# Polysketch attention and a squared-ReLU layer on one core: another layout for v, the weights loaded as float32 and cast on the chip, the key features on GpSimd

## The chip, the core and the metric

The kernel runs on one core of one Trainium2 chip. Its engines work from queues of their own: TensorE (PE) multiplies matrices into PSUM, VectorE (DVE) and ScalarE (ACT) work element by element and read PSUM, GpSimd (POOL) works element by element on SBUF alone, and SyncE (SP) issues DMAs. An instruction starts when it is first in its engine's queue and what it waits for is done. The metric is the device time of one execution in microseconds (us); lower is better.

## The reference

Four batches with four heads of 1,088 tokens, 32 numbers each; S1 and S2 are 8 x 32.

```python
def phi(x):                                    # 32 numbers -> 64 features
    a = einsum('rd,bhsd->bhsr', S1, x)
    b = einsum('rd,bhsd->bhsr', S2, x)
    return einsum('bhsi,bhsj->bhsij', a, b).reshape(*x.shape[:-1], 64)
q_p, k_p = phi(q), phi(k)
kv  = einsum('bhsf,bhsd->bhfd', k_p, v)        # per batch and head 64 x 32
z   = sum(k_p, axis=2)
num = einsum('bhsf,bhfd->bhsd', q_p, kv)
den = einsum('bhsf,bhf->bhs', q_p, z) + 1e-6
x   = (num / den) as 4352 tokens x 128         # the heads side by side
h   = x @ w_in                                 # 128 x 2048
out = (max(h, 0) ** 2) @ w_out                 # 2048 x 128
```

## The kernel before

**Staging.** The 34 x 32 tokens of a head lie as 32 partitions of 34 tokens, so that a tile of k or q is [128 = 4 heads x 32, 34, 32] and comes with one DMA of 544 KB. v is laid out by tokens instead: four DMAs of 32 partitions bring 8 tokens each per head, and two more the tokens left over. All of these are issued on SP, batch by batch (`load`). The two weights come by DMAs of GpSimd that turn them into bfloat16 on the way (`w_in_sb`, `w_out_sb`); a copy of one element ahead of each makes it wait for the last piece of v of batch 0, and for q of batch 1.

**Keys.** `kT` transposes k in 32 x 32 blocks on DVE, `ka` multiplies by S1 and S2 on PE, `kc` copies the result out of PSUM on ACT, `kp` forms the 64 products of a token on DVE, and `kv` sums products times v over the tokens on PE. `kt` copies the sums to SBUF, `kr` turns them upright with a matmul against the identity, `kx` copies them to `KV`. The tokens of k and of v must be the same in each group of rows: in `kT` row and column follow the layout of v. `kg`, `gs`, `wz` and `wc` give the sums for the denominator.

**Queries.** `qT` transposes q on DVE, `qa` multiplies on PE, `qc` copies; `dt`, `dr`, `da` make the denominator's reciprocal and scale; `qf` forms the products and `qp` transposes them, all on DVE. `nd` multiplies them with `KV` on PE (32 x 32 matmuls, sixteen at a time in the array), and `xe` copies the result as bfloat16, which gives x transposed.

**The layer.** The tokens go in nine chunks, eight of 512 and one of 256 columns. For chunk `ci` and pair `u` of eight, `M` makes two 128 x 512 results of x and w_in in one of two PSUM buffers, `R` takes the ReLU of both (128 x 1024) on ACT or DVE, `S` squares them on DVE or ACT (with `@M` two pairs at once), and `O` adds their products with w_out, eight matmuls of 128 columns, to one PSUM buffer. `E` copies a chunk's result, and four DMAs of SP store it.

**The order.** One text, `ORDER`, lists every operation, as `name.arguments@engine`; `pin` keeps the order of the program, so each engine's queue is the order of its operations in that text. In names here, kp.1.0 is the first half of batch 1, M.0.5 is chunk 0 and pair 5. `W.n` puts n idle matmuls (128 x 128 x 512) into PE's queue; before, the text has none, and eight stand ahead of it in the program.

Of the kernel before, what the change touches and what calls it, by code (L numbers as in the profile page):

```python
# [10 lines left out]
F32 = mybir.dt.float32  # L11
BF16 = mybir.dt.bfloat16
# [58 lines left out]
def kernel(  # L71
# [11 lines left out]
    nc = tc.nc  # L83
# [6 lines left out]
    NLO = 8  # L90
# [49 lines left out]
    for b in range(B):  # L140
        kin_t[b] = kin.tile([128, NJ, D], F32, tag=f"k{b}", name="k_in")
        qin_t[b] = kin.tile([128, NJ, D], F32, tag=f"q{b}", name="q_in")
        vraw[b] = vin.tile([128, H, NLO + 1, D], F32, tag=f"v{b}", name="v_in")


    def load(b):
        for dst, src in ((kin_t, k), (qin_t, q)):
            nc.sync.dma_start(out=dst[b], in_=src[b].rearrange("h (t j) d -> (h t) j d", j=NJ))
        vb = v[b].rearrange("h (t j) d -> t h j d", j=NJ)
        for i in range(4):  # L150
            nc.sync.dma_start(  # L151
                out=vraw[b][32 * i : 32 * (i + 1), :, :NLO, :].rearrange("t h l d -> t h (l d)"),
                in_=vb[:, :, i * NLO : (i + 1) * NLO, :].rearrange("t h l d -> t h (l d)"),
            )
        for j2 in range(2):
            nc.sync.dma_start(
                out=vraw[b][32 * j2 : 32 * (j2 + 1), :, NLO, :], in_=vb[:, :, 4 * NLO + j2, :]
            )


# [4 lines left out]
    w_in_sb = consts.tile([128, d_ff], BF16)  # L165

    pin(nc.gpsimd.tensor_copy(w_in_sb[:1, :1], vraw[0][:1, 0, NLO, :1]))
    nc.gpsimd.dma_start(out=w_in_sb, in_=moe_w_in)

    w_out_sb = consts.tile([128, C_TILES, 128], BF16)  # L170
    pin(nc.gpsimd.tensor_copy(w_out_sb[:1, 0, :1], qin_t[1][:1, 0, :1]))
    nc.gpsimd.dma_start(out=w_out_sb, in_=moe_w_out.rearrange("(c ct) d -> c ct d", ct=C_TILES))
# [91 lines left out]
    def kT(b, i, eng):  # L264
        if i == 0:
            T["kT", b] = kTp.tile([128, S], F32, tag="kT", name="kT")
        kt, src = T["kT", b], kin_t[b]
        l0, l1 = (4 * i, 4 * i + 4) if b == 0 else (0, NLO)
        pin(
            nc.vector.transpose(  # L270
                kt[:, 128 * l0 : 128 * l1].rearrange("p (l h t) -> p l h t", h=4, t=32),
                src[:, : 4 * NLO, :].rearrange("p (h l) d -> p l h d", h=4)[:, l0:l1],
            )
        )
        if b == 0 and i == 0:
            return
        pin(
            nc.vector.transpose(  # L278
                kt[:, 1024:].rearrange("p (j t) -> p j t", j=2), src[:, 4 * NLO :, :]
            )  # L280
        )
# [112 lines left out]
    def kr(b, eng):  # L394
        T["kr", b] = t = ps_m.tile([128, 512], F32, tag="m", name="kr_ps")
        for f in range(2):
            pin(
                nc.tensor.matmul(
                    t[:, 128 * f : 128 * f + 128],
                    T["kvT", b][:, f].rearrange("p c i -> p (c i)"),  # L400
                    ident,
                    start=True,
                    stop=True,
                )
            )
# [207 lines left out]

    def M(ci, u, eng):
        N = columns(ci)
        T["h", ci, u] = t = ps_h.tile([128, 2, 512], F32, tag="h", name="h_ps")
        for i in range(2):
# [3 lines left out]
                    w_in_sb[:, 2 * u + i :: C_TILES],  # L621
# [32 lines left out]
    def O(ci, u, eng):  # L654
# [3 lines left out]
        for i in range(2):  # L658
            ct = 2 * u + i
            for m in range(nt):  # L660
# [4 lines left out]
                        w_out_sb[:, ct, :],  # L665
# [28 lines left out]
    OPS.update(W=W, M=M, R=R, S=SQ, O=O, E=E)  # L694
# [34 lines left out]
```

## Time and profile before

| | us |
|---|---|
| median of the 3 runs (113.83 to 116.07) | 114.15 |
| the profiled execution | 112.86 |
| its span, first to last instruction | 111.1 |
| busy: PE, DVE, ACT, POOL | 98.9, 94.5, 84.3, 2.2 |
| PE from the first M to the last O | 21.1 to 106.8 |
| last O to the end of the span (copy, last DMA) | 4.3 |

A line of a group in the profile reads: line of the kernel, engine, operation, tiles written and read, shapes, count, then the busy time together and the mean of one in ns, then the idle time of the engine ahead of them and what ended it. In a timeline the columns are start, length, engine, line. PE's matmuls are pipelined: what one costs in a row of equals is the distance from start to start and not its length. A line of stages begins with the two ends in us and the length.

### The profile page before, as it was taken

What the parts mean: (1) busy time and instruction counts of PE and PEld (TensorE: products, weight loads), DVE (VectorE), ACT (ScalarE), POOL (GpSimd) and SP (SyncE); (2) the same over time, 40 slices, a digit from 0 to 9 for tenths busy, and PEclk for the clock granted to TensorE, in tenths of its full rate; (3) what the DMA queues carried; (4) which work ended last, traced back from release to release, by engine and by line L of the source; (5) the groups of instructions that cost most, each with busy time, mean ns of one, the idle gap of its engine ahead of it and who ended that gap; (6) DMA issues with size and microseconds to landing.
All of it is one profiled execution on the core that took longest, in us unless ns stands there. A gap on an engine that the chain in (4) does not pass through costs nothing.

```text
span 111.1 us, 4158 instructions
## 1 busy us (share of the span) xinstructions
PE 98.9 (89%) x1817; PEld 77.3 (70%) x1835; DVE 94.5 (85%) x149; ACT 84.3 (76%) x138; POOL 2.2 (2%) x10
## 2 busy tenths in 40 slices
PE   5786788599999999999999999999999999989940
PEld 2165676256868878777788678888767887879830
DVE  5479946975999999999999999999959999988900
ACT  3331023379999999999999997999989779957730
POOL 2000320000000000000000000000000000000000
PEclk9999557959999999999999999999999999999998
DMA  3899999999990000300400003040030021031031
GB/s 96 239 238 213 280 212 304 284 254 210 305 179 3 6 3 6 94 0 6 94 6 0 0 6 94 0 97 3 6 81 13 6 67 27 0 74 32 5 89 53
DMA packets 6691, 10.24 MB, mean 92 GB/s; under 512 B 2193, under 2 KB 4369, under 8 KB 6673
## 3 DMA queue, kind: packets, MB, share of 16 engines
q1 hardware_dynamic: 6224, 8.85, 32.0%
q0 software_dynamic: 288, 1.05, 4.8%
q8 instruction: 14, 0.23, 0.9%
q10 hardware_dynamic: 160, 0.07, 0.2%
q14 instruction: 5, 0.03, 0.1%
HBM read 8.79 MB, written 2.23 MB: 99 GB/s over the span
## 4 chain that ended last, share of the span: by engine, by line
PE 59%; DMA 16%; ACT 14%; issue 3%; SPq 2%; DVE 1%; POOL 0%; ACTq 0%
PE o_ps L662 22%; PE h_ps L619 22%; ACT r_sb L639 10%; DMA w_in_sb<-in_moe_w_in_dram 8%; DMA v_in<-in_v_dram 7%; PE nd_ps L583 3%; PE kab_ps L293 3%; PE qab_ps L447 3%; PE acc_ps L374 3%; ACT g_sb L650 2%; SPq L151 2%; DMA out_dram<-osb 2%; PE h_ps L583 1%; ACT xT L607 1%; ACT osb L674 1%
## 5 line engine op out<-in xcount | busy, mean ns | idle before, releaser
L639 ACT ACTIVATE r_sb<-h_ps 128x1024 bf16<-128x1024 f32 (+1 forms) x67 | 62.8, 1005 | 7.4 <-PE h_ps L619 4.7
L662 PEld LDWEIGHTS <-g_sb 128*128 128x128 bf16 x544 | 34.0, 98 | 8.2 <-issue 0.6
L619 PE MATMUL h_ps<-xT,w_in_sb 128*128 128x512 bf16 (+1 forms) x126 | 37.7, 381 | 2.0 <-DMA w_in_sb<-in_moe_w_in_dram 1.3
L652 DVE TENSOR_TENSOR g_sb<-r_sb 128x1024 bf16<-128x1024 bf16 (+2 forms) x44 | 39.1, 925 | 0.3
L662 PE MATMUL o_ps<-w_out_sb,g_sb 128*128 128x128 bf16 x544 | 38.0, 219 | 0.5
L619 PEld LDWEIGHTS <-w_in_sb 128*128 128x128 bf16 x144 | 16.7, 149 | 5.0 <-issue 2.4
L323 DVE TENSOR_TENSOR kp<-kab 128x1024 f32<-128x1024 f32 (+1 forms) x8 | 10.6, 1336 | 0.0
L551 DVE STREAM_TRANSPOSE qp<-qf 128x1024 f32<-128x1024 f32 (+1 forms) x9 | 10.4, 1175 | 0.2
L538 DVE TENSOR_TENSOR qf<-aq,qab 128x1024 f32<-128x1024 f32 (+1 forms) x9 | 10.4, 1157 | 0.1
L583 PE MATMUL h_ps<-qp,KV 32*32 32x256 f32 (+2 forms) x224 | 8.2, 321 | 0.0
L583 PE MATMUL nd_ps<-qp,KV 32*32 32x256 f32 (+2 forms) x224 | 8.1, 321 | 0.0
L293 PEld LDWEIGHTS kab_ps<-Wk,kT 128*64 128x64 f32 x136 | 5.2, 149 | 2.8 <-issue 1.1
L583 PEld LDWEIGHTS nd_ps<-qp,KV 32*32 32x32 f32 x224 | 5.1, 110 | 2.4 <-DVE g_sb L652 0.8
L293 PE MATMUL kab_ps<-Wk,kT 128*64 128x64 f32 x136 | 6.0, 238 | 0.9 <-DVE kT L278 0.5
L374 PE MATMUL acc_ps<-kp,v_in 128*32 128x64 f32 x288 | 5.8, 244 | 0.9 <-DMA v_in<-in_v_dram 0.9
L374 PEld LDWEIGHTS acc_ps<-kp,v_in 128*32 128x32 f32 x288 | 5.1, 125 | 2.2 <-PE cz_ps L469 1.0
L641 DVE TENSOR_SCALAR r_sb<-h_ps 128x1024 bf16<-128x1024 f32 (+1 forms) x5 | 5.1, 1010 | 0.8 <-PE h_ps L619 0.6
L674 ACT COPY osb<-o_ps 128x512 f32<-128x512 f32 (+1 forms) x9 | 5.2, 581 | 0.6 <-PE o_ps L662 0.5
L417 DVE STREAM_TRANSPOSE qT<-q_in 128x512 f32<-128x512 f32 x8 | 5.2, 682 | 0.3 <-DMA q_in<-in_q_dram 0.3
L270 DVE STREAM_TRANSPOSE kT<-k_in 128x1024 f32<-128x1024 f32 (+1 forms) x5 | 5.0, 1017 | 0.0
L447 PEld LDWEIGHTS qab_ps<-Wq,qT 128*64 128x64 f32 x96 | 4.1, 137 | 1.1 <-issue 0.8
L311 ACT COPY kab<-kab_ps 128x256 f32<-128x256 f32 (+1 forms) x12 | 3.4, 320 | 1.9 <-PE kab_ps L293 1.8
(69 smaller groups left out, 68.8 us busy)
## 6 DMA issues: line engine op xcount, KB each, us to landing
k_in<-in_k_dram SPq DMA_DIRECT2D x4, 544.0 KB, 3.8
q_in<-in_q_dram SPq DMA_DIRECT2D x4, 544.0 KB, 6.8
out_dram<-osb SPq DMA_DIRECT2D x33, 64.0 KB, 1.7
v_in<-in_v_dram SPq DMA_DIRECT2D x16, 128.0 KB, 7.1
w_in_sb<-in_moe_w_in_dram POOLq DMA_DIRECT2D x1, 512.0 KB, 8.7
w_out_sb<-in_moe_w_out_dram POOLq DMA_DIRECT2D x1, 512.0 KB, 9.8
v_in<-in_v_dram SPq DMA_DIRECT2D x8, 16.0 KB, 6.7
out_dram<-osb ACTq DMA_DIRECT2D x1, 64.0 KB
```

Of the source, the lines that this page charges most:

```text
L293: nc.tensor.matmul(kk[64 * c : 64 * c + 64, m * 64 : (m + 1) * 64], kt[:, c0 + 64 * c : c0 + 64 * c + 64], Wk.rearrange("p h x -> p (h x)" ...
L323: tt.tensor_tensor(out=t[:, :n], in0=s[:, 0, :n, :, None].to_broadcast([128, n, r, r]), in1=s[:, 1, :n, None, :].to_broadcast([128, n, r, r]),
L374: nc.tensor.matmul(acc[32 * h : 32 * h + 32, :64], vraw[b][:, h, 4 * gi + m, :], t[:, m * H + h].rearrange("p i j -> p (i j)"), start=(gi ...
L447: nc.tensor.matmul(t[64 * c : 64 * c + 64, m * n : (m + 1) * n], cols, Wk.rearrange("p h x -> p (h x)") if not b else Wq[:, be].rearrange( ...
L538: nc.vector.tensor_tensor(out=t[:, :n], in0=T["aq", b][:, g0 : g0 + n, :, None].to_broadcast([128, n, r, r]), in1=T["qab", b][:, g0 : g0 + ...
L551: nc.vector.transpose(T["qp", b][:, :, 128 * i : 128 * i + 32 * nm].rearrange("p f (m t) -> p m f t", t=32), T["qf", b, i][:, : nm * H].re ...
L583: nc.tensor.matmul(nds[l][32 * h : 32 * h + 32, d0 : d0 + n], KV[rows, be[l // 2], f, 32 * h : 32 * h + 32], src[rows, 2 * h + f, c0 : c0 ...
L619: nc.tensor.matmul(t[:, i, :N], w_in_sb[:, 2 * u + i :: C_TILES], T["x", ci][:, :N], start=True, stop=True,)
L639: pin(nc.scalar.activation(t, h, ACTF.Relu))
L652: pin(nc.vector.tensor_mul(t, s, s))
L662: nc.tensor.matmul(T["o", ci][:, m, :], T["g", ci, u // 2][:, 2 * (u % 2) + i, m * 128 : (m + 1) * 128], w_out_sb[:, ct, :], start=(ct == ...
L674: pin(COPY[eng](osb[:, :nt], T["o", ci][:, :nt]))
```

## The change

- **v.** A head's tokens are taken in 64 runs of 17: two DMAs a batch bring 9 and 8 tokens of each run to partitions 0 to 63 and 64 to 127. `kT` now makes two transposes, each writing every second column, where it made one.
- **Weights.** `w_in` and `w_out` come as float32 on SP, between the loads of batch 1, and are cast in four pieces each by `ci` and `co`: seven on GpSimd, `ci.1` on ACT. GpSimd issues no DMA any more.
- **Key features.** All eight `kp` are on GpSimd.
- **kr.** The two float32 matmuls against the identity are transposes.
- **The order.** `ORDER` is another text: the operations stand elsewhere, seven idle matmuls lie ahead of M.0.0, and some copies, squares and ReLUs change engine: E from nine on ACT to seven and two on DVE, kx from three to one on ACT, S from four to two, R from 67 to 68.

```diff
+wk.0 bp.0 kT.0.0 ka.0.0 kT.0.1 bd.0 kc.0.0 ka.0.1 kc.0.1 W.2 kg.0 qT.0 qa.0.0 gs.0@V wz.0 wc.0
+qc.0.0@V wq.0 W.1 cz.0 dt.0.0 dr.0.0 qa.0.1 qc.0.1@A kT.1.0 da.0.0 cz.1 kp.0.0@G kv.0.0 dt.0.1
+kp.0.1@G W.2 kv.0.1 ci.3@G qf.0.0 qp.0.0 kt.0 ci.0@G ka.1.0 ka.1.1 kc.1.0 kc.1.1 kp.1.0@G kr.0
+kx.0@A kg.1 gs.1@A W.1 nd.0 qT.1 ci.1@A xe.0.0@V xe.0.1@A wz.1 W.1 M.0.0 R.0.0@A M.0.1 dr.0.1
+R.0.1@A wc.1 da.0.1 qf.0.1 qa.1.0 qa.1.1 qc.1.0@A qc.1.1@A kp.1.1@G S.0.0@V ci.2@G M.0.2 R.0.2@A
+M.0.3 R.0.3@A kv.1.0 kv.1.1 kt.1 qp.0.1 nd.1 dt.1.0 xe.1.0@A M.0.4 kT.2.0 ka.2.0 ka.2.1 xe.1.1@A
+co.2@G R.0.4@A co.1@G co.0@G kc.2.0 M.0.5 M.0.6 kc.2.1 dr.1.0 S.0.3@M S.0.1@V O.0.0 R.0.5@A kg.2
...
     def load(b):
         for dst, src in ((kin_t, k), (qin_t, q)):
+            if b == 1 and src is q:
+                nc.sync.dma_start(out=w_in_raw, in_=moe_w_in)
             nc.sync.dma_start(
+                out=dst[b][:, :NJ], in_=src[b].rearrange("h (t j) d -> (h t) j d", j=NJ)
+            )
+        if b == 1:
             nc.sync.dma_start(
+                out=w_out_raw, in_=moe_w_out.rearrange("(c ct) d -> c (ct d)", ct=C_TILES)
+            )
+        vb = v[b].rearrange("h (p l) d -> p h l d", l=17)
+        for c, n in ((0, 9), (1, 8)):
+            nc.sync.dma_start(
+                out=vraw[b][64 * c : 64 * c + 64, :, :n, :].rearrange("p h l d -> p h (l d)"),
+                in_=vb[:, :, 9 * c : 9 * c + n, :].rearrange("p h l d -> p h (l d)"),
+            )
...
-    pin(nc.gpsimd.tensor_copy(w_in_sb[:1, :1], vraw[0][:1, 0, NLO, :1]))
-    nc.gpsimd.dma_start(out=w_in_sb, in_=moe_w_in)
...
+        for j2 in range(2):
+            pin(
+                nc.vector.transpose(
+                    kt[:, 128 * l0 : 128 * l1].rearrange("p (l c t j) -> p j l c t", c=2, j=2, t=32)[:, j2],
+                    src[:, 17 * j2 : 17 * j2 + 18]
+                    .rearrange("p (c l) d -> p l c d", c=2)[:, l0:l1],
+                )
+            )
...
-                nc.tensor.matmul(
+                nc.tensor.transpose(
                     t[:, 128 * f : 128 * f + 128],
                     T["kvT", b][:, f].rearrange("p c i -> p (c i)"),
                     ident,
-                    start=True,
-                    stop=True,
                 )
...
+    def ci(p, eng):
+        src = w_in_raw.rearrange("d (c ct) -> d ct c", ct=C_TILES)
+        pin(COPY[eng](w_in_sb[p], src[:, 4 * p : 4 * p + 4]))
+
+    def co(p, eng):
+        src = w_out_raw.rearrange("c (ct d) -> c ct d", ct=C_TILES)
+        pin(COPY[eng](w_out_sb[p], src[:, 4 * p : 4 * p + 4]))
...
-                    w_in_sb[:, 2 * u + i :: C_TILES],
+                    w_in_sb[u // 2][:, 2 * (u % 2) + i, :],
```

## The prediction

> **What bounds the kernel now.** I read the slices of the span first, then the chain that ended last, then the sums by stage, then the rows of the operations that change place. The slices, forty of 2.78 us each:
>
> ```profile
> PE   5786788599999999999999999999999999989940
> DVE  5479946975999999999999999999959999988900
> ACT  3331023379999999999999997999989779957730
> PEclk9999557959999999999999999999999999999998
> DMA  3899999999990000300400003040030021031031
> GB/s 96 239 238 213 280 212 304 284 254 210 305 179 3 6 3 6 94 0 6 94 6 0 0 6 94 0 97 3 6 81 13 6 67 27 0 74 32 5 89 53
> ```
>
> There are two regimes. Up to about 22 us the DMA engines are full while PE, DVE and ACT wait in turn, with TensorE's clock halved in three slices and at 0.7 in one. From 25 us on the three engines are full together, and the loads end near 33 us. The sums by stage (windows of 5 us) show that ACT is as tight there as PE:
>
> ```profile
> 35.00:40.00 5.00, 4.95 (x62) 4.31 (x62) 4.93 (x9) 5.00 (x9) 0.00 (x0) 1.00 0.02 3
> 60.00:65.00 5.00, 4.85 (x110) 3.60 (x110) 4.96 (x8) 5.00 (x10) 0.00 (x0) 1.00 0.01 3
> ```
>
> The columns after the length are PE, weight load, DVE, ACT, POOL, clock, DMA share and GB/s. A busy PE is not a PE at its peak, so I measure PE by its pitch, read from the chain in order of time where nothing interrupts it:
>
> ```profile
> 73.98 0.44 PE h_ps L619 x2
> 74.42 0.45 PE o_ps L662 x8
> ```
>
> So an M (two matmuls) costs 0.44 and an O (eight) 0.45. In the same way ka costs 0.57 and 0.64 (first and second half of a batch), qa 0.76, kv 1.13 a batch, kr 0.45, kg 0.31, wz 0.2, nd 0.9 (batch 0) to 1.45. In the order written out, what follows M.0.0 is 81.1 us of PE by these prices: M 29.9, O 30.6, ka 3.1, qa 4.8, kv 3.4, kr 1.35, kg 0.9, wz 0.6, nd 6.5. M.0.0 starts at 21.09 and the last O ends at 106.77, so 85.7 were taken and 4.6 lost: about half at the halved clock before M.0.5 (28.59, where 75.7 are left), 2.5 after it. The last copy and its DMA take 4.3.
>
> The start and the queue of loads, from the timeline:
>
> ```profile
> 5.10 0.43 SPq L148 DMA_DIRECT2D k_in<-in_k_dram  x1
> 8.52 0.35 SPq L148 DMA_DIRECT2D q_in<-in_q_dram  x1
> 13.42 0.35 SPq L148 DMA_DIRECT2D k_in<-in_k_dram  x1
> 21.09 1.41 PE L619 MATMUL h_ps<-xT,w_in_sb 128*128 128x512 bf16 x3 [1.30 <-DMA w_in_sb<-in_moe_w_in_dram]
> ```
>
> The loads are issued in order on SP, and an issue waits for the landing of the one eight places earlier: q of batch 1 goes out at 8.52 when q of batch 0 lands, k of batch 2 at 13.42 when k of batch 1 lands. M.0.0 waits 1.30 us for w_in; its x was ready at 19.5.
>
> **What moves off DVE and ACT.** The rows, by shape:
>
> ```profile
> L639 ACT ACTIVATE r_sb<-h_ps 128x1024 bf16<-128x1024 f32 x61 | 59.5, 1045 | 6.2 <-PE h_ps L619 4.2 <-remote 1.6 <-PE acc_ps L374 0.2
> L323 DVE TENSOR_TENSOR kp<-kab 128x1280 f32<-128x1280 f32 x4 | 5.9, 1466 | 0.0
> L323 DVE TENSOR_TENSOR kp<-kab 128x1024 f32<-128x1024 f32 x4 | 4.8, 1206 | 0.0
> L674 ACT COPY osb<-o_ps 128x512 f32<-128x512 f32 x8 | 4.9, 608 | 0.1
> masks.py:199 POOL TENSOR_SCALAR_AFFINE_SELECT ident<-ident 128x128 f32<-128x128 f32 x1 | 0.3, 287 | 0.1
> L167 POOL CAST w_in_sb<-v_in 1x1 bf16<-1x1 f32 x1 | 0.2, 176 | 10.5 <-DMA v_in<-in_v_dram 10.5
> ```
>
> All eight kp leave DVE: 4 x 1.206 + 4 x 1.466 = 10.7 us. DVE takes two E (0.6), two kx, two qc, one xe and two more S, and gives up one R: about +4. ACT loses two E (0.61 each), two kx (0.4), two qc (about 0.45), one xe (0.8), two S (1.09) and gains an R and ci.1. Summed by the new order, ACT's work from M.0.0 to nd.2 (the products of batch 1) falls from 24.0 to 22.5, and from nd.2 to the end from 67.0 to 63.8. These are sums of means; neighbours overlap (61 x 1.045 = 63.7 against 59.5 busy), so I take 0.93 of them. For before this gives 22.3 for M.0.0 to nd.2, and 21.09 to 43.37 were measured: ACT set that stage. After: 20.9.
>
> **On GpSimd.** No row has a product there. From the CAST of one element and the select of 128, one element costs (287 - 176)/127 = 0.87 ns. With that slope once, kp costs 1.07 and 1.29 us; with 287/128 = 2.24 ns an element, 2.30 and 2.87. I take the slope twice, for two inputs: 1.96 and 2.40. A cast of 512 elements is between 0.62 and 1.15 us; I take 0.62, as it is the same operation as the CAST row. The Trainium skill (GPSIMD Engine Reference, Elementwise — side-by-side cycle accounting) gives 4497 ns for a 2048-element product; by it a kp would cost, as an estimate, 2.25 and 2.85, kp.1.1 below would end 0.8 later, still before v1, and the sum would be the same.
>
> **Loads.** All now stand in one SP queue: k0 q0 v0 v0 k1 w_in q1 w_out v1 v1 k2, and so on. With 18 loads on SP instead of 32, the eight-places rule holds w_out only for k0 and k2 only for v0, so nothing is issued late; the bytes decide. Summed over the slices, the kernel before has moved 3.28 MB (k0 to w_in) at 15.4 us, 3.83 (q1) at 17.6, 4.88 (w_out) at 21.2, 5.44 (v1) at 23.2 and 6.0 (k2) at 25.5. Landings come behind their bytes: q0's are reached at 6.1 and it landed at 8.5, v0's at 8.6 and 11.9, k1's at 11.3 and 13.4. With 2.1 to 2.3 us of lag: w_in 17.5, q1 19.7, w_out 23.3, v1 25.5, k2 27.7. Before, q1 landed at 15.6 and k2 at 22.4. The v rows (1,152 and 1,024 bytes against 1,024, the 128-byte pieces gone) I cost at nothing: v0 is needed at 13.7, after kp.
>
> **The new start.** DVE: qT.0 from 8.5 (q0's landing) to 10.1, then gs, wc and qc.0.0 to 11.3, dt.0.0 and dr.0.0 to 12.5. Next stands kT.1.0, waiting for k1 until 13.4; its two 128x512 transposes and the rest (2 x 0.68 + 0.2, against 1.24 + 0.2) end at 15.0. Behind it wait da, dt.0.1, qf.0.0 and qp.0.0 (0.29 + 0.28 + 1.22 + 1.23): 18.0, against 15.1 before. Writes at every second element have no row; a transpose at twice its price would put DVE 1.3 later here, still ahead of q1. PE: kv.0 ends near 16, ka.1 17.2, kr.0 18, nd.0 19.3, where kp on GpSimd (7.0 to 8.9 and to 11.3) is long done. The seven idle matmuls are 0.22 to 0.43 each in gaps and cost nothing. Then qT.1, put ahead of xe.0.0 on DVE, waits for q1: 19.7 + 1.54, xe.0.0 + 0.54, so M.0.0 at 21.9 instead of 21.1. GpSimd, where kp.1.0 and kp.1.1 stand behind ci.3 and so behind w_in too, has cast ci.3 and ci.0 by 18.7 (19.8 at the upper price), so the cast is hidden behind qT.1 and would cost only what it runs past 21.8.
>
> **The next wait.** kv.1 needs v1 (25.5) and kp.1.1 (23.1; 25.0 at the upper price), and PE reaches it at about 25.3, held by ACT's R. O.0.0 needs co.0 (25.6, or 29.6) and comes at about 31. So GpSimd's price doesn't count up to its upper end. ka.2.0 needs kT.2.0: k2 at 27.7 + 1.56 = 29.3, and PE stands idle for about 2 us. After ka.2 (1.2), M.0.5 starts at 30.5. By then the new order has also done qa.1 and kv.1 (1.52 + 1.13), which came after M.0.5, and three kr by transposes save half of 0.45 each (the transpose of L211 has one record where a kr matmul has two): 72.4 us are left. 30.5 + 72.4 = 102.9, against 28.59 + 75.7 = 104.3: 1.4 gained. Of the 2.5 lost after this point in before I take 0.8 away, since ACT has 3 us less to do after nd.2 (bounds 0 and 2.5). **Sum: -2.2 us**, between -1.4 and -3.9. The profiled run took 112.86 (span 111.1 and 1.76 around it), 1.1% below the median 114.15 of the runs shown; I put the difference on the median: **111.9 us**.
>
> **Rivals.** *Loads without the lag.* One queue of few, large pieces may land with its bytes: q1 17.6, k2 25.5. Then M.0.0 comes at 20.2 behind qp.0.0, M.0.5 at 28.3, 3.6 instead of 1.4 gained, and with 0.8 to 2.5 of the later loss 4.4 to 6.1 in all: about 109.2. For it: k0, alone on the engines, landed at 4.5, its bytes being reached at 4.0. Against it: q0, too, was a large piece and lagged 2.4.
>
> *GpSimd and DVE shut each other out* (slower). DVE has only 0.8 us to spare: its sum from M.0.0 to qp.1.1 is 20.0, so 21.8 to 41.8, while PE is ready for nd.2 at 30.5 + 12.1 = 42.6. In that stretch GpSimd has 9.9 us (three kp, five casts) beside S, qf, da and dt, which read two SBUF inputs. If DVE waits for half of it, nd.2 is 4.1 later than forecast: -2.2 + 4.1 = +1.9; if for all, +6.9. It is slower than before once DVE waits for more than 3.0 of the 9.9. No trace of before has both engines at work, so nothing speaks for or against it by a number; it costs 1 to 5% with the middle at +3, 117.2. The Trainium skill (SBUF — State Buffer, Who interferes with whom) has this as a rule: a DVE instruction with two SBUF inputs and a GpSimd instruction that reads SBUF exclude each other for the whole instruction. By that rule the +1.9 to +6.9 would come; no run so far can show it.
>
> *The weights land slowly.* The packets of q1 took 32.0% of the span for 8.85 MB, 4.0 us a MB; the weights' queue q0 4.8% for 2.1 MB read, 2.5. At q1's rate the two weights take 3.1 us more, k2 lands at 30.8, and the sum is +0.9: 115.0.
>
> **How the numbers follow.** Chances: forecast 0.34, loads without lag 0.22, shut-out 0.29, slow weights 0.15. A measurement here tells about 2% (2.3 us). The forecast's own range, 110.3 to 112.8, lies half on each side of that line: faster 0.22 + 0.18 = 0.40; slower 0.19 of the shut-out and 0.05 of slow weights = 0.24; the rest, 0.36, is within 2%. The range runs from 108.0 (loads without lag, all of the loss gone) to 117.2 (the shut-out's middle).
>
> **What would show it.** Right: M.0.0 waits on xT from DVE behind q1, not on w_in; a PE gap of 1 to 2 us before ka.2 that ends with k2; kp on POOL near 2 us; qf and S on DVE at 1.2 as before. Wrong: those two rows longer, or POOL's far above 2.9 (shut-out); q1 before 18 us (no lag); k2 after 30 (slow weights); an ACT still full to 65 us, which would leave the 2.5 us in place.

## The result: 6% slower

| | before | after |
|---|---|---|
| median of the runs, us | 113.99 (4 runs, 113.01 to 116.07) | 121.06 (4 runs, 120.25 to 123.98) |
| the profiled execution; its span | 112.86; 111.1 | 121.58; 119.5 |
| busy: PE, DVE, ACT, POOL | 98.9, 94.5, 84.3, 2.2 | 105.1, 96.1, 82.3, 26.9 |
| M.0.0 starts; M.0.5 | 21.09; 28.6 | 22.17; 38.35 |
| nd.2 starts; nd.4 | 43.37; 62.6 | 50.88; 69.4 |

The kernel after takes 1.0627 times as long as before, with a 95% interval of 1.0495 to 1.0759. (On this core some executions of any kernel take 1.5 to 4% longer than the rest; the ratios here leave them out, and where too few others were left, the range of the runs stands alone.) Of the 8.4 us between the two spans, 7.5 are there when nd.2 starts.

The slices of the kernel after, forty of 2.99 us each, to be laid beside those of before:

```profile
PE   5799997909939999999559999999999999999970
DVE  5362697795992459999999999999997989988740
ACT  4012115623607899989539999999998978997870
POOL 2029444995000980009900000000000000000000
PEclk9999999985595899999999999999999999999997
DMA  3999999999930000030030001301201200303031
```

PE is full sooner than before (from the third digit, the idle matmuls counted), then falls to 0 at the ninth digit, 24 to 27 us, and to 3 at the twelfth; its clock is halved just behind each of these. A second dent, 5 and 5, lies at 57 to 63 us, where ACT falls to 5 and 3 as well, and there the clock is full. These are two different losses.

**The first loss: PE waits, and for nothing that another engine does.** The timeline of PE in the kernel after (start, length, instruction; in brackets the idle time ahead of it and what ended it):

```profile
22.17 1.02 PE L633 MATMUL h_ps<-xT,w_in 128*128 128x512 bf16 x4
23.12 0.88 PE L452 MATMUL qab_ps<-Wq,qT 128*64 128x96 f32 x15
27.06 1.70 PE L452 MATMUL qab_ps<-Wq,qT 128*64 128x96 f32 x17 [3.06 <-issue]
30.52 2.15 PE L381 MATMUL acc_ps<-kp,v_in 128*32 128x64 f32 x72
...
35.26 0.29 PE L588 MATMUL nd_ps<-qp,KV 32*32 32x128 f32 x1 [1.87 <-issue]
```

qa.1 stops after 15 of its matmuls and goes on 3 us later with the same inputs. "issue" says that the profile knows of no semaphore that it waited for. There are three such stops: in ka.1 at 17.54 (1.06 us to the next record), in qa.1 at 23.75 (3.31) and in nd.1 at 33.13 (2.13). In the trace's list of PE's records (weight loads, matmuls and those of its sequencer together) they stand behind records 449, 705 and 961: exactly 256 apart. Queue q8, which the page of the profile calls "instruction", moves its packets of 16,384 bytes just then, and each stop ends 1.4 to 1.5 us after one of them is done. So I read these stops as PE having run out of instructions; the experiments below test it.

From these records, in us. A new block of 256 is entered, and in the same moment the fetch of the next can begin; the fetch's packets start and end; the next block is needed, which is where the last record of the old one starts:

| | entered | fetch | wait to its start | needed | PE stops for |
|---|---|---|---|---|---|
| before | 10.43 | 13.63 to 14.99 | 3.2 | 17.39 | 0 |
| | 17.39 | 20.72 to 21.68 | 3.3 | 25.34 | 0 |
| | 25.34 | 26.77 to 28.05 | 1.4 | 31.75 | 0 |
| after | 12.61 | 16.12 to 17.22 | 3.5 | 17.54 | 1.06 |
| | 18.60 | 24.16 to 25.59 | 5.6 | 23.75 | 3.31 |
| | 27.06 | 32.56 to 33.88 | 5.5 | 33.13 | 2.13 |
| | 35.26 | 36.40 to 37.77 | 1.1 | 43.47 | 0 |

Two things have changed. While the loads run, a block lasts 4.9 to 6.1 us in the kernel after and 6.4 to 8 in before; the new order leaves PE fewer gaps. And the fetch starts later while the loads run: the last load lands at 35.6, and from then on the wait is 1.1 us or less and no stop is left. The Trainium skill (Runtime: NRT & Kernel Launch, Instruction fetch mechanics) has the block of 256 instructions and 16 KiB, which this trace shows, and says that the cost of crossing one is "mostly hidden"; here three crossings cost 6.5 us.

The windows of 5 us behind the stops (PE, weight load, DVE, ACT, POOL, clock, DMA share, GB/s):

```profile
25.00:30.00 5.00, 2.94 (x21) 1.84 (x21) 3.72 (x5) 1.19 (x3) 3.47 (x4) 0.60 1.06 263
30.00:35.00 5.00, 3.39 (x108) 2.36 (x106) 4.93 (x9) 2.08 (x3) 0.00 (x0) 0.72 0.81 152
35.00:40.00 5.00, 4.74 (x73) 3.06 (x74) 1.50 (x4) 3.02 (x9) 0.88 (x1) 0.66 0.02 4
```

The clock is 0.60, 0.72 and 0.66, where before had 0.99, 1.00 and 1.00 in the same three windows. At that clock kv.1 took 2.08 us (1.13 in before) and ka.2 2.12 (1.21), so the stops are followed by a second loss. But the clock was halved for as long in before, 10.2 us in each of the two profiles: at 11.4 to 18.3 and 21.7 to 25.1 there, at 26.0 to 32.8 and 36.3 to 39.7 here. How much of the 8.4 us the clock makes is therefore not shown.

**The second loss: DVE and GpSimd.** Rows by shape (count, busy us, mean ns, idle before), first two of before, then three of the kernel after:

```profile
L652 DVE TENSOR_TENSOR g_sb<-r_sb 128x2048 bf16<-128x2048 bf16 x21 | 24.9, 1205 | 0.0
L525 DVE TENSOR_TENSOR aq<-qab,den 128x256 f32<-128x256 f32 x3 | 1.2, 404 | 0.0
```

```profile
L666 DVE TENSOR_TENSOR g_sb<-r_sb 128x2048 bf16<-128x2048 bf16 x23 | 30.7, 1357 | 4.7 <-ACT r_sb L653 4.6
L530 DVE TENSOR_TENSOR aq<-qab,den 128x256 f32<-128x256 f32 x3 | 2.2, 719 | 0.1
L330 POOL TENSOR_TENSOR kp<-kab 128x1280 f32<-128x1280 f32 x4 | 9.8, 2450 | 20.3 <-issue 20.3
```

A mean hides it; single instructions show it. The timeline of DVE, and that of GpSimd, around the second dent:

```profile
54.31 3.42 DVE L666 TENSOR_TENSOR g_sb<-r_sb 128x2048 bf16<-128x2048 bf16 x1
58.52 1.31 DVE L530 TENSOR_TENSOR aq<-qab,den 128x256 f32<-128x256 f32 x1
```

```profile
8.19 4.32 POOL L330 TENSOR_TENSOR kp<-kab 128x1024 f32<-128x1024 f32 x2 [6.89 <-ACT kab L318]
...
54.05 5.50 POOL L330 TENSOR_TENSOR kp<-kab 128x1280 f32<-128x1280 f32 x2 [9.64 <-issue]
```

The square that begins at 54.31, just behind a kp, takes 3.42 us instead of 1.2. Meanwhile the reduction and the reciprocal on DVE, which have one input, keep their lengths (0.44 and 0.35). GpSimd pays too: the pair of kp takes 4.32 us at the start, where DVE mostly transposes, and 5.50 here. DVE's next ReLU comes late, and PE waits for it, as PE's timeline shows:

```profile
61.02 0.81 PE L633 MATMUL h_ps<-xT,w_in 128*128 128x512 bf16 x3 [2.16 <-DVE r_sb L655]
```

### The profile page after: what moved, and what is told of

It is laid out like the page before. It is cut to its first block, busy times and chain, and to the rows that moved or that the text cites. A ratio compares the mean times of both kernels' runs of the same rounds, so it can differ in the third digit from the quotient of the medians.

```text
span 119.5 us, 4166 instructions
## 1 busy us (share of the span) xinstructions
PE 105.1 (88%) x1834; PEld 74.7 (63%) x1834; DVE 96.1 (80%) x155; ACT 82.3 (69%) x130; POOL 26.9 (23%) x21
## 4 chain that ended last, share of the span: by engine, by line
PE 67%; DVE 20%; issue 6%; DMA 3%; ACTq 0%; ACT 0%
PE h_ps L633 21%; PE o_ps L676 19%; DVE g_sb L666 10%; PE qab_ps L452 5%; PE kab_ps L300 5%; PE acc_ps L381 4%; DVE qp L556 4%; PE nd_ps L588 4%; PE idle_ps L195 3%; DMA S<-in_S_dram 3%; DVE qf L543 2%; PE cz_ps L474 2%; PE h_ps L588 1%; DVE aq L530 1%; PE gg_ps L345 1%
## 5 line engine op out<-in xcount | busy, mean ns | idle before, releaser
L666 DVE TENSOR_TENSOR g_sb<-r_sb 128x2048 bf16<-128x2048 bf16 (+2 forms) x46 | 44.2, 999 | 5.3 <-ACT r_sb L653 5.1
L633 PE MATMUL h_ps<-xT,w_in 128*128 128x512 bf16 (+1 forms) x144 | 40.5, 380 | 2.2 <-DVE r_sb L655 2.2
L676 PE MATMUL o_ps<-w_out,g_sb 128*128 128x128 bf16 x544 | 38.7, 219 | 0.4 <-DVE g_sb L666 0.4
L330 POOL TENSOR_TENSOR kp<-kab 128x1024 f32<-128x1024 f32 (+1 forms) x8 | 19.4, 2448 | 30.4 <-issue 20.3
L633 PEld LDWEIGHTS <-w_in 128*128 128x128 bf16 x144 | 11.9, 100 | 8.8 <-issue 5.7
L452 PE MATMUL qab_ps<-Wq,qT 128*64 128x96 f32 x96 | 5.6, 271 | 3.1 <-issue 3.1
L195 PE MATMUL idle_ps<-idle 128*128 128x512 bf16 x15 | 6.8, 561 | 1.2 <-DVE mask L133 1.2
L300 PE MATMUL kab_ps<-Wk,kT 128*64 128x64 f32 x136 | 7.1, 271 | 0.8 <-issue 0.8
L300 PEld LDWEIGHTS kab_ps<-Wk,kT 128*64 128x64 f32 x136 | 6.3, 181 | 1.7 <-issue 1.0
L276 DVE STREAM_TRANSPOSE kT<-k_in 128x512 f32<-128x512 f32 (+1 forms) x10 | 5.2, 571 | 0.0
```

The source lines that it names most:

```text
L195: pin(nc.tensor.matmul(T["idle"], idle[:, :128], idle, start=True, stop=True))
L300: nc.tensor.matmul(kk[64 * c : 64 * c + 64, m * 64 : (m + 1) * 64], kt[:, c0 + 64 * c : c0 + 64 * c + 64], Wk.rearrange("p h x -> p (h x)" ...
L330: tt.tensor_tensor(out=t[:, :n], in0=s[:, 0, :n, :, None].to_broadcast([128, n, r, r]), in1=s[:, 1, :n, None, :].to_broadcast([128, n, r, r]),
L452: nc.tensor.matmul(t[64 * c : 64 * c + 64, m * n : (m + 1) * n], cols, Wk.rearrange("p h x -> p (h x)") if not b else Wq[:, be].rearrange( ...
L633: nc.tensor.matmul(t[:, i, :N], w_in_sb[u // 2][:, 2 * (u % 2) + i, :], T["x", ci][:, :N], start=True, stop=True,)
L666: pin(nc.vector.tensor_mul(t, s, s))
```

## The experiments

Two theories came out of this: **F**, the fetch of PE's instructions stands late behind the queued loads; and **S**, the shut-out: GpSimd's products and DVE's operations with two inputs exclude each other. The expectations use these letters where they use any. All times are medians in us; the ratio is to the kernel before as it ran beside that kernel, with its 95% interval. Where a range stands in place of a ratio, it is that of the kernel's own four runs, and such a row can't be placed more closely than 2 to 4%. The column of before differs by up to 1.7%, so rows are compared by their ratios.

| kernel | us | before | ratio |
|---|---|---|---|
| after | 121.06 | 113.99 | 1.0627 [1.0495, 1.0759] |
| few_loads_before | 111.66 | 112.41 | 0.9895 [0.9798, 0.9992] |
| few_loads_after | 116.25 | 112.41 | 1.0400 [1.0253, 1.0547] |
| kp_on_dve | 122.96 | 112.41 | runs 119.16 to 124.00 |
| order_alone | 118.09 | 112.41 | 1.0544 [1.0448, 1.0641] |
| kp_gpsimd_before | 125.96 | 113.55 | 1.1042 [1.0862, 1.1221] |
| casting_dma_after | 122.48 | 113.55 | runs 119.26 to 123.54 |
| v17_before | 113.61 | 113.55 | 1.0014 [0.9963, 1.0065] |
| kr_before | 113.36 | 113.55 | runs 110.88 to 114.36 |
| memset_kp_after | 117.38 | 113.76 | 1.0222 [1.0055, 1.0390] |
| small_loads_after | 116.45 | 113.76 | 1.0237 [1.0126, 1.0348] |
| memset_kp_few_loads | 107.97 | 113.76 | 0.9527 [0.9424, 0.9631] |
| small_loads_memset | 111.39 | 114.28 | 0.9831 [0.9740, 0.9921] |
| small_kp23_dve | 116.23 | 114.28 | runs 113.54 to 116.42 |
| small_kp123_dve | 115.62 | 114.28 | 1.0288 [1.0192, 1.0384] |
| before_small | 114.91 | 114.28 | 1.0059 [0.9958, 1.0159] |

### Fewer loads, in both kernels

Both kernels leave out the loads of batches 2 and 3 and compute these from the tiles of batches 0 and 1:

```diff
+        if b >= 2:
+            kin_t[b], qin_t[b], vraw[b] = kin_t[b - 2], qin_t[b - 2], vraw[b - 2]
+            continue
...
-    for b in range(B):
+    for b in range(2):
         load(b)
```

> The changed kernel without the loads of batches 2 and 3 (it computes them from the tiles of batches 0 and 1; 3.3 MB less to load, all else as it was). Theory F: with less queued on the DMA engines the blocks of code come earlier, the pause at 33.1 us goes and that at 23.8 shrinks under 1.5 us, TensorE's clock stays full from 26 us on, the products of batch 2 move from 50.9 to about 45, run 114 to 117. Theory L: nothing of this depends on loads that nobody waits for; run 120 to 122. Theory O (the order itself is at fault): as L.

> The control for the run without the loads of batches 2 and 3: the kernel before, with the same loads left out. Theory F: its blocks of code already arrive in time or behind other waits, so it gains 0 to 1.5 us (112.5 to 114). If it gains as much as the changed kernel does, the loads cost both alike and explain nothing of the difference.

Against before the kernel after falls from 1.063 to 1.040, and before itself to 0.990; the intervals are a point or more wide to each side, so the times alone say little. The profiles say more. PE's stops shrink from 1.06, 3.31 and 2.13 to 0.73, 1.12 and none, and M.0.5 starts at 29.23 instead of 38.35; before has no such stop with its loads or without. F is at work, then, and in the kernel after. But 4.6 us still lie between the two medians. In few_loads_after PE now waits elsewhere; its sum of waits and the timeline of DVE:

```profile
PE o_ps L679 <- DVE g_sb L669: 4.1, 2, 3.8
```

```profile
30.36 2.63 DVE L533 TENSOR_TENSOR aq<-qab,den 128x256 f32<-128x256 f32 x1
33.02 2.87 DVE L546 TENSOR_TENSOR qf<-aq,qab 128x1024 f32<-128x1024 f32 x1
```

Both run beside a pair of kp on GpSimd (30.00 to 34.80), at 6.5 and 2.4 times their lengths in before (0.40 and 1.22), and the squares that O needs stand behind them: S. With the loads gone this pair, the kp of batch 2, ran 9 us earlier than in after, where it had met one square and lengthened it by 0.9.

### The key features back on DVE

```diff
-... kp.0.0@G kv.0.0 dt.0.1 kp.0.1@G ... kp.1.0@G ... kp.1.1@G ... kp.2.1@G ... kp.2.0@G ... kp.3.1@G ... kp.3.0@G
+... kp.0.0 kv.0.0 dt.0.1 kp.0.1 ... kp.1.0 ... kp.1.1 ... kp.2.1 ... kp.2.0 ... kp.3.1 ... kp.3.0
```

> The changed kernel with its eight key products on VectorE again, nothing else moved. Theory L (GpSimd and VectorE shut each other out, and this is what costs): VectorE's long rows go (aq of 128x128 from a mean of 1139 ns back to 290, the squares of 3422 and 2120 ns to 1200), but VectorE takes 10.7 us more; run 118 to 120. Theory F (TensorE waits for its own instructions, because the blocks of code arrive late behind the loads): the pauses of 3.3 us at 23.8 and 2.1 us at 33.1 stay, run 120 to 123.

Its runs (119.16 to 124.00) and those of the kernel after (120.25 to 123.98) overlap: no gain is shown. The order of the kernel after has kp.0.0 behind gs, wc, qc, dt, dr, kT.1.0 and da on DVE's queue, where DVE waits for PE twice (1.50 and 1.37 us); kp.0.0 starts at 15.64, PE stops for 4.31 us ahead of kv.0, and M.0.0 starts at 25.59. This run exchanges one wait for another and can't weigh S by itself. It does show that GpSimd's casts lengthen DVE's operations too: beside those of 13.54 to 16.61 da took 0.82 us and kp.0.0 2.05, where order_alone, which has no casts, had 0.25 and 1.22 in the same place. The stops of F shrink to 1.20 and 1.15, since PE, held up elsewhere, reaches its blocks later.

### One part at a time, in the kernel before

The order alone (kp on DVE, no ci and co, everything else as before):

```diff
-wk.0 wq.0 kT.0.0 ka.0.0 kT.0.1 bp.0 bd.0 kc.0.0 kp.0.0 ka.0.1 kc.0.1 kg.0 gs.0@A qT.0 wz.0 wc.0
+wk.0 bp.0 kT.0.0 ka.0.0 kT.0.1 bd.0 kc.0.0 ka.0.1 kc.0.1 W.2 kg.0 qT.0 qa.0.0 gs.0@V wz.0 wc.0
+qc.0.0@V wq.0 W.1 cz.0 dt.0.0 dr.0.0 qa.0.1 qc.0.1@A kT.1.0 da.0.0 cz.1 kp.0.0 kv.0.0 dt.0.1
...
```

> The kernel before with the new order text alone: its own loads, its weights by casting DMAs, the layout of v, the matmuls of kr and the key products on VectorE as before. Theory O: the order is at fault by itself, run 119 or more. Theories F and L: neither the deep queue of loads nor GpSimd's work is there; TensorE's pauses at the ends of code blocks stay under 1.5 us each, run 113 to 116.5.

The key features on GpSimd alone:

```diff
-... kp.0.0 ka.0.1 kc.0.1 ... kp.0.1 ... kp.1.1 ... kp.1.0 ... kp.2.0 ... kp.2.1 ... kp.3.1 ... kp.3.0
+... kp.0.0@G ka.0.1 kc.0.1 ... kp.0.1@G ... kp.1.1@G ... kp.1.0@G ... kp.2.0@G ... kp.2.1@G ... kp.3.1@G ... kp.3.0@G
```

> The kernel before with the eight key products on GpSimd, nothing else: the shut-out by itself, with neither the deep queue of loads nor the new order. Theory L: aq, qf and the squares that meet a product on GpSimd take up to 2.9 us instead of 0.3 to 1.2, which eats what VectorE saves (10.7 us of products); 0 to +3 us against before. Without a shut-out: VectorE 10.7 us lighter, all rows as before, -1 to -3 us.

v in runs of 17 (its two DMAs a batch, the transposes of `kT`):

```diff
-        vb = v[b].rearrange("h (t j) d -> t h j d", j=NJ)
-        for i in range(4):
+        vb = v[b].rearrange("h (p l) d -> p h l d", l=17)
+        for c, n in ((0, 9), (1, 8)):
...
+        for j2 in range(2):
...
```

> The kernel before with v in runs of 17 tokens alone (two loads a batch instead of six, two transposes of half size instead of one for k). Theory F: six loads fewer a batch let SP issue earlier, so more bytes wait on the DMA engines; the blocks of code may come later, +0 to +2 us. If the layout is harmless: -1 to +1 us.

kr by transposes:

```diff
-                nc.tensor.matmul(
+                nc.tensor.transpose(
                     t[:, 128 * f : 128 * f + 128],
...
-                    start=True,
-                    stop=True,
```

> The kernel before with the sums turned by transposes alone: half of 0.45 us for each of four kr, one of them ahead of the first M; -0.7 to 0 us against before, at the edge of what can be measured. All theories agree.

v17_before changes nothing that can be measured. For kr_before the runs lie too far apart to tell an effect of up to 2%. (The kr matmuls fall from 16 records of 3.1 us busy to 8 of 1.8.) v17_before has a stop of its own, 2.39 us at record 449: with its fewer and larger pieces the first fetch waits 5.1 us where before had 3.2. It paid nothing for it in the end, so a stop need not cost its length.

The order alone costs 5.4%, but this order was made for kp on GpSimd: PE waits for kp.0 (2.14 us at 13.03), and later 2.3 us for qp and 0.7 for a square, both on DVE. One stop of F is there, 1.12 us at 29.18.

kp on GpSimd alone costs 12 us, far more than expected. PE's waits there, and GpSimd's timeline:

```profile
PE acc_ps L374 <- POOL kp L323: 7.1, 2, 5.8
PE o_ps L662 <- DVE g_sb L652: 4.6, 2, 2.4
```

```profile
14.99 0.18 POOL L171 CAST w_out_sb<-q_in 1x1 bf16<-1x1 f32 x1 [2.70 <-DMA q_in<-in_q_dram]
15.47 0.53 POOL L172 DMA_DIRECT2D w_out_sb<-in_moe_w_out_dram  x1 [0.31 <-POOL w_out_sb L171]
16.02 4.32 POOL L323 TENSOR_TENSOR kp<-kab 128x1024 f32<-128x1024 f32 x2
```

7.1 us are a queue: in before's program the two DMAs of the weights stand ahead of ORDER on GpSimd, and the second waits for q of batch 1, so kp.0.0 can't begin before 16.02. The other 4.6 fit S: DVE's squares took 1437 and 790 ns (128x2048 and 128x1024) against 1205 and 680: 21 x 0.232 + 22 x 0.110 = 7.3 us of DVE's time. In before's order, moving the weights off GpSimd is thus a condition of moving kp there.

### The weights by casting DMAs in the kernel after

```diff
-                nc.sync.dma_start(out=w_in_raw, in_=moe_w_in)
...
+    nc.gpsimd.dma_start(out=w_in_sb, in_=moe_w_in)
```

(and w_out likewise; no ci, no co)

> The changed kernel with the weights as before, by GpSimd's casting DMAs into bfloat16, and no casts on the engines; order, layout of v, kr and key products as changed. Theory F: the two weights (2.1 MB) leave SP's queue, and at the time of the pauses at 23.8 and 33.1 us little else changes in bytes, so the pauses shrink to about 1 us each as they did in the run with the new order alone; first M at 21 to 22, run 115 to 118. Theory L or O: run 119 to 122, since neither is touched.

119.26 to 123.54, where 115 to 118 was expected of F. The stop in qa.1 is gone (its fetch waited 2.4 us instead of 5.6), that in nd.1 is still there (1.9 us waited), and PE waits 3.0 us for kp.0, which again stands behind the weights' DMAs on GpSimd. So this run also pays one thing with another and can't tell what the way of the weights costs by itself.

### Each cause by itself

Fills instead of products, so that GpSimd is busy for as long but reads next to nothing (one element for each kp); the kernel leaves out the key features:

```diff
-        pin(tt.tensor_tensor(out=t[:, :n], in0=..., in1=..., op=ALU.mult))
+        pin(nc.gpsimd.tensor_copy(t[:1, 0, 0, :1], s[:1, 0, n - 1, :1]))
+        pin(nc.gpsimd.memset(t[:, :n], 1.0))
+        pin(nc.gpsimd.memset(t[:, :n], 1.0))
```

> The kernel after, but each kp on GpSimd is replaced by a copy of one element of kab (so that it still waits for the features) and two fills of the whole kp tile with 1. The products of the key features are left out; GpSimd stays busy at the same places for about as long (a fill of 128x128 takes 0.2 us in the trace of before, so I estimate 2 x 1.0 to 1.1 us against 1.96 and 2.40 for kp), but reads no SBUF while it fills. Theory S (GpSimd's products and the two-input operations of DVE shut each other out): the long rows of DVE go (no g_sb 128x2048 over 1.6 us, no qf over 1.4, no aq over 0.6), and with them about 2 to 4 us of the time: 117 to 119.5. Theory F (TensorE waits for its instruction blocks behind the queued loads): nothing of F changes, the pauses of 3.3 and 2.1 us stay. If F alone makes the loss, 120.5 to 122. If both act, 117 to 119.5 with the pauses still there.

The two fills take 0.95 and 1.17 us each, so that GpSimd is as busy as before the edit (24.7 us against 26.9). The ratio is 1.022 instead of 1.063: S goes and F stays. A row of DVE by shape, and PE's waits:

```profile
L661 DVE TENSOR_TENSOR g_sb<-r_sb 128x2048 bf16<-128x2048 bf16 x23 | 27.5, 1216 | 4.9 <-ACT r_sb L648 4.8
```

```profile
PE qab_ps L447 <- issue: 2.8, 1, 2.8
PE kab_ps L300 <- issue: 2.6, 1, 2.6
PE nd_ps L583 <- issue: 2.4, 1, 2.4
```

Squares are back at 1216 ns, DVE's busy time falls from 96.1 to 90.1 us, and between nd.2 and nd.4 the time falls from 18.55 to 15.28: S cost 3.3 us there. Ahead of nd.2 1.5 us are gained, although the stops are longer (2.83, 3.04 and 2.69 instead of 1.06, 3.31 and 2.13). All that PE still waits for, beyond the start, is its own instructions, 7.8 us of it.

The loads in small pieces, with nothing left out:

```diff
-            nc.sync.dma_start(
-                out=dst[b][:, :NJ], in_=src[b].rearrange("h (t j) d -> (h t) j d", j=NJ)
-            )
+            for h in range(H):
+                nc.sync.dma_start(
+                    out=dst[b][32 * h : 32 * h + 32, :NJ],
+                    in_=src[b, h].rearrange("(t j) d -> t j d", j=NJ),
+                )
```

(v two heads at a time, each weight in four pieces of 512 columns)

> The kernel after with every load on SP cut into pieces: k and q one head a piece (136 KB), v two heads a piece (144 and 128 KB), the weights in four pieces of 256 KB. The order of the bytes is unchanged. As an issue waits for the landing of the one eight places earlier, at most eight pieces or 1.1 to 2 MB are outstanding, where after has up to eight of 0.5 to 1 MB (about 4 to 5 MB). Theory Q, a sharper form of F (a block of TensorE's instructions is fetched through the same DMA engines and stands behind what the loads have queued there): the wait from the request to the fetch falls from 5.6 and 5.5 us to 2 to 4, as in before (3.3 to 1.1), the pauses of 3.3 and 2.1 us to under 1, the halved clock behind them goes, and the time falls by 3 to 6 us, 115 to 118. If the fetch waits because the engines are full, whatever is queued, it starts as late as in after, and the time stays at 120 to 122. 64 issues of 0.43 us on SP may delay the loads themselves by 1 to 2 us.

116.45 (1.024), as F's sharper form has it. The waits from the request to the fetch are 3.3, 3.3 and 3.5 us instead of 3.5, 5.6 and 5.5, though all bytes are still loaded and the last load lands later (39.3 against 35.6). So the fetch does not wait for the loads to end. What changed is how much is under way at a time, at most eight pieces of mostly 128 to 144 KB instead of eight of 256 KB to 1 MB. The fourth wait is only 1.4 us (from 29.38), though loads still run. PE's waits in small_loads_after:

```profile
PE kab_ps L307 <- issue: 2.3, 1, 2.3
PE h_ps L640 <- DVE r_sb L662: 2.2, 1, 2.2
PE nd_ps L595 <- issue: 1.8, 1, 1.8
```

The stop of 3.31 is 0.5 now, and M.0.5 starts at 32.38 instead of 38.35. Two stops remain (2.56 at 14.93 and 2.02 at 27.36): a fetch of 3.4 us of waiting, 1.2 of packets and 1.5 until PE goes on needs blocks of 6 us, and these two last 3.5 and 4. The middle line is S, unchanged.

Both, in a kernel with fewer loads and in one with all of them:

> The same replacement of kp by fills, and the loads of batches 2 and 3 left out as in few_loads_after (their work is done on the tiles of batches 0 and 1). Both suspected causes are gone. Theory F and S together make up the loss: the time comes down to that of few_loads_before, 111.7 (span 108.5), or below, since the engines' sums of the kernel after are smaller: 107 to 111. If something third costs (the order itself, the writes at every second column, a late cast), it stays at 113 to 116 and the trace shows where TensorE waits.

> Both remedies in a kernel with all its loads: the loads in pieces as in small_loads_after, and the fills in place of kp as in memset_kp_after (the products of the key features are left out). If the two causes add and there is no third: 121.1 - 4.6 (small_loads_after) - 3.7 (memset_kp_after) = 112.8, or less, since the pauses left over in small_loads_after (2.6 and 2.0 us) are partly at the queue's mercy: 110 to 113. The 108.0 of memset_kp_few_loads stays out of reach by the loads that are kept. If both remedies help by the same way (less of a backlog at one place), 115 to 116.5.

107.97 and 111.39. The second closes the account. Against before, after stands at +6.3%; small pieces take off 3.9 points, the fills 4.05, together 7.95; both in one kernel took off 7.96. (The intervals are about a point wide to each side, so that close an agreement is luck.) Within them the two causes add and the account needs no third: without them, and without the products, the kernel after is 1.7% faster than before. nd.2 starts at 43.20.

### Is there a version that beats both?

Small pieces, and the kp of batches 2 and 3, or of 1 to 3, back on DVE:

```diff
-... kp.2.1@G ... kp.2.0@G ... kp.3.1@G ... kp.3.0@G
+... kp.2.1@V ... kp.2.0@V ... kp.3.1@V ... kp.3.0@V
```

```diff
-... kp.1.0@G kr.0 ... xe.0.0@V ... kp.1.1@G
+... kr.0 ... xe.0.0@V kp.1.0@V ... kp.1.1@V
```

> small_loads_after with the four kp of batches 2 and 3 on DVE, at the places where they stood; the four of batches 0 and 1 stay on GpSimd. Theory S: in small_loads_after a g_sb 128x2048 took 3.42 us at 48.64 beside a pair of kp (48.31 to 53.88 on GpSimd) against 1.21 to 1.22 in memset_kp_after, and aq 128x256 1.31 against 0.42; these go. DVE gets 2 x 1.21 + 2 x 1.47 = 5.3 us of products back, of which the lock had already cost it about 3 to 4, and is busy for about 97 of 111 us. I expect -1 to -3 us: 113.5 to 115.5, same as before. If the lock costs nothing on the path, DVE only has more to do: 116.5 to 119.

> As small_kp23_dve, with the two kp of batch 1 on DVE too (kp.1.0 behind xe.0.0, kp.1.1 at its place), so that GpSimd has only the two of batch 0, in the start where DVE does transposes with one input, and seven casts. Theory S: another 2.7 us on DVE between M.0.0 and kv.1, against a lock of 1 to 2 there; kv.1 waits for kp.1.1 by up to 1 us. 113 to 116. If the kp of batch 1 were the dear ones, below small_kp23_dve by over 1 us; if GpSimd is of use there, above it by 1 to 2.

small_kp123_dve stands at 1.029, small_loads_after at 1.024: no gain. small_kp23_dve can't be placed: one run took 113.54, the other three 116.17 to 116.42. The long rows go (128x2048 squares at 1.209 and 1.208 us), but DVE has 5.4 or 8.0 us of products back. Its busy time is 96.8 us in both, against 95.6 in small_loads_after: the 8.0 us of products had cost DVE 6.8 from GpSimd. Now DVE lags by itself. PE's waits in small_kp123_dve:

```profile
PE nd_ps L595 <- DVE qp L563: 2.7, 2, 1.6
PE nd_ps L595 <- ACT r_sb L660: 1.2, 1, 1.2
```

No version with all its work was shown to be faster than before. Last, small pieces in the kernel before:

```diff
-            nc.sync.dma_start(out=dst[b], in_=src[b].rearrange("h (t j) d -> (h t) j d", j=NJ))
+            for h in range(H):
+                nc.sync.dma_start(out=dst[b][32 * h : 32 * h + 32], in_=src[b, h].rearrange("(t j) d -> t j d", j=NJ))
```

> The kernel before with k and q of each batch in four pieces of 136 KB. Theory Q: before shows no pause of TensorE without a semaphore, so the shorter queue gains nothing through the fetches: -1 to +1 us, 112.5 to 115. If small pieces speed the loads themselves (k and q in smaller parts, landing sooner), the start gains too: M.0.0 before 20.5 instead of 21.1, 110 to 112.

The kernel before, with k and q in small pieces, stays where it was (1.006). Its fetches waited no shorter either (3.8 and 3.5 us against 3.2 and 3.3), and its profile, of one of the longer runs, has two short stops, 0.67 and 1.28 us, where before has none. Small pieces are no gain as such; in the kernel after they are one.

## Why the prediction was wrong, point by point

**What held.** A pair of kp takes 4.32 us where nothing hinders it, against 1.96 + 2.40 = 4.36 by the slope taken twice. (The Trainium skill, in GPSIMD Engine Reference, Elementwise — side-by-side cycle accounting, has 4497 ns for a `tensor_tensor` of 2048 numbers, measured with an add; in proportion that gives 2.25 and 2.81 as an estimate, not 2.85, and is 15 and 17% above.) M.0.0 came at 22.17 against 21.9, though not for the reason given: q of batch 1 had been transposed by 20.3, and M.0.0 waited for nd.0, which the first stop had made late. The layout of v costs nothing, as priced; what the transposes of kr bring can't be told. And the sum itself is near what the change is worth without the two causes: 0.980 of before was forecast, 0.983 measured in small_loads_memset, with M.0.5 at 31.3 against 30.5 and nd.2 at 43.2 against the 42.6 for which PE was to be ready. That hit is partly luck: k of batch 2 landed at 27.7 there, as the sum has it, but in small pieces and not in the large ones that it was worked out for.

**The step that failed: "the next wait".** It had PE at kv.1 at about 25.3, an idle time of 2 us behind k of batch 2, and M.0.5 at 30.5. The loads were not late: w_in landed at 14.10 (17.5 in the sum), w_out at 20.56 (23.3), v of batch 1 at 23.15 (25.5), k of batch 2 at 24.82 (27.7), so that the first rival, loads without the lag, was right in its landings. (The lag of 2.1 to 2.3 us that the sum took had left out v of batch 0, whose rows there say 3.3.) But kv.1 started at 30.52 and M.0.5 at 38.35. The step counted semaphores, data and engines, and PE waited for its own instructions: 3.31 and 2.13 us between M.0.0 and M.0.5, then half the clock, which added 0.95 to kv.1 and 0.91 to ka.2 and about 1.7 to qa.1 and the two M between 27.06 and 30.52. So the overlap that the step took for granted, PE's work against the fetch of its own instructions, is the term that it put at nothing. No rival had this mechanism. In before it can be read: the queue is on the page,

```profile
q8 instruction: 14, 0.23, 0.9%
```

and its fetches wait 3.2 and 3.3 us there as well; only the length of a block, 7 to 8 us, covers them. A denser order with larger loads takes that cover away from both sides.

**The slower rival: right in kind, near the low end in size, and later than put.** GpSimd and DVE do shut each other out. The rival had DVE wait for half to all of 9.9 us between M.0.0 and nd.2, which against the forecast is 4.1 to 9.1 us. DVE lost 6.0 us in all (96.1 against 90.1 busy), and the time 4.05 points of before, some 4.6 us (1.0627 against 1.0222). Of the 4.8 that the profiled executions show, 1.5 arose ahead of nd.2, in part hidden by the stops, and 3.3 behind it, beside the kp of batch 3, where the step had looked at no overlap. small_loads_after, which has this cause in full and some of the other, stands at 116.45, within the range given; the rest of F put the time beyond. The rule of the Trainium skill that the prediction named (SBUF — State Buffer, Who interferes with whom) agrees with the runs: operations of DVE with two inputs in SBUF lengthen beside a kp, up to 3.42 us from 1.2, and not beside a fill, which reads nothing. Beside a cast, which reads SBUF too, they lengthen as well (kp.0.0 of kp_on_dve, 2.05 from 1.22).

**The slow weights** did not occur. The casts, priced at 0.62 us, took 0.975 (w_out) and 1.067 (w_in) in the mean; PE waited for none of them.

**What stays open.** Small pieces shorten the fetch's wait in the kernel after and not in before, so what sets it is not shown. It does not simply follow the bytes under way: by the issues and landings of the kernel after these were about 4.6 MB at 12.61 (a wait of 3.5 us), 3.8 at 18.60 (5.6) and 2.8 at 27.06 (5.5). Whether the fetch stands in the same queue of a DMA engine or is only served more slowly, no run tells apart. How much of the loss is the stops and how much the halved clock isn't separated. Nor was it tried to hold the loads of batches 2 and 3 back until PE's blocks last longer.

## What to carry to other kernels

A fully unrolled kernel has one more input that no semaphore shows: PE's instructions came 256 at a time in these traces, asked for one block ahead, and a fetch waited longest while large loads were under way. There, count what PE has to do in a block against the wait for a fetch (3.3 us here behind pieces of some 140 KB, up to 5.6 behind pieces of 256 KB to 1 MB, then 2.6 more until PE goes on); an order that packs PE more densely, or fewer and larger loads, can turn a hidden fetch into a stop. And work given to GpSimd was free only beside what DVE does with one input: six of the products, 8.0 us on DVE, cost DVE 6.8 us from there.

## What the runs showed of the hardware that was not expected

- PE's longer stops without a semaphore stand 256 records apart, give or take a few that a trace lacks, and end 1.2 to 1.6 us after a packet of 16,384 bytes on the instruction queue.
- A fetch waited up to 5.6 us while large loads were under way, 1.2 to 3.5 while small ones were (kernel after), and up to 1.6 with none.
- The clock was at 0.60 to 0.72 in the windows behind the stops of 3.31 and 2.13 us, and stayed at 1.00 (20 to 25 us) behind the one of 1.06. A stop of 2 to 3 us did not always bring this: the clock stayed full behind one of 2.29 (15.31 to 17.60 in memset_kp_few_loads) and one of 2.56 (14.93 to 17.48 in small_loads_after).
- A square on DVE (128x2048) took up to 3.42 us beside GpSimd's products and 1.216 in the mean in the kernel with GpSimd's fills, which are about as long but read nothing.
- GpSimd's cast of 512 float32 a partition took 0.62 us from a contiguous source when undisturbed (w_out in memset_kp_after), and 1.0 to 1.1 from every sixteenth element (w_in).
